# Masked attention and a max-out FFN on one core: first loads moved into the command list, V and w0 loads split, all commands ordered anew

## The chip, the core and the metric

The kernel runs on one NeuronCore of one Trainium2 chip. A core has five engines with an instruction stream each: TensorE (PE, matrix products and transposes), VectorE (DVE), ScalarE (ACT), GpSimd (POOL) and SyncE (SP, which here only issues transfers). Transfers between device memory and the on-chip memory SBUF are issued by SP, ACT or POOL and carried out by 16 DMA engines. The engines run beside each other and wait for each other by semaphores. Products land in PSUM banks and are copied or combined from there.

The metric is device time in microseconds of one execution; 8 runs of the kernel before are given.

## What is computed

Attention over 4 batches of 8 heads, 768 positions of width 64, and then a feed-forward net over the 3072 rows of 512 that come of it. Some heads (the "retrieval" heads, a flag each, read at run time) see all earlier positions; the others see the first 4 positions and the last 64.

```python
scores = scale * np.matmul(q, k.transpose(0, 1, 3, 2))
stream_keep = causal & (is_sink | in_win)          # n_sink = 4, window = 64
mask = np.where(retr, full_mask, stream_mask)      # by head
scores = np.where(mask[None], scores, -1e9)
a = np.exp(scores - max); a = a / sum(a)
x = np.matmul(a, v)                                # to (3072, 512)
h = np.maximum(np.maximum(x @ w1, x @ w2), x @ w3) # (3072, 768)
out = h @ w_out                                    # (3072, 512)
```

## The kernel before

**Tiles.** Work is cut into 16 tiles t, in the order batch, half of the 768 positions, group of four heads: t = 4 * batch + 2 * half + group. Each tile has two head pairs i = 0, 1. Scores are made transposed (keys on partitions), so that exp(scores) can be used at once as the stationary operand of the product with V; a column of ones in V gives the sums. Blocks of a tile are packed into units u (2 for the first half, 4 for the second; `UNITS`). Each half of a batch, 384 rows, is then one FFN pass: 8 passes in all.

**The order is written by hand, as a list of commands.** `PROGRAM` (L46) is a tuple of strings; at the end of the kernel each command is looked up in `do` (L647) and emits its instructions. Since every engine runs its own instructions in the order in which they were emitted, the list sets the order on every engine and on every transfer queue, and a letter in a command says which engine does a copy (`a` ACT, `d` VectorE, `p` POOL). The commands:

- `hl half hp n` (`load_first`, L298) loads k and q of n head pairs of batch 0 in fp32, from pair hp on, on SP and ACT. Before the change it can stand only in `FIRST` (L44), which is run ahead of all set-up; so does `v b half` there, and `ir`, the load of the flags.
- `ld half hp` does the same for two pairs on POOL's queue. `cast half hp ee` turns k and q of a pair into fp16 (`cast_pair`, L207; tiles kn, qn). `turnp half hp e` transposes them on PE and copies them out of PSUM into KQ (`turn_pair`, L219). This way is for batch 0 alone.
- `load b qd` loads k and q of four heads of a later batch on POOL's queue, with conversion; `turn b qd i part` transposes a quarter of them on VectorE (L258, L266).
- `load_v b half` loads V by three transfers on SP, `load_vp` on POOL (`load_v`, L280; its last two arguments pick a range of heads). `v t i ee` (`prep_v`, L497) casts V into va (L503) and makes vf (L505), V with far positions switched off for the other heads.
- `read`, `flags`, `far` spread the flags; `em hp` and `m hp` (`head_masks`, L386) make a pair of heads' mask tiles mk on VectorE (L388). Tiles 0 and 1 add the masks on PE before the exponential (L536), later ones multiply them in afterwards: `k t i u e` (`masks`, L569).
- `s t u [i] [b]` (`scores`, L517) makes the scores of a unit on PE (L552) and their exponential on ACT (L563). Two PSUM tiles named st serve in turn; with `b`, single banks are used.
- `av t i [D]` (`av`, L589): product with V (L601), reciprocal and scaling on VectorE (L609, L611). With `D` the result x is transposed by a DMA on SP (L620), otherwise by PE and a copy (`x t i e`, `turn_x`, L626). The last `x` of a half puts its FFN pass into a queue.
- `f 1 e` takes the next step of the FFN pass at the head of the queue (`ffn`, L416): 18 steps of four products of 384 columns (L437), which are copied (w0) or combined by maximum on VectorE (w1, w2; L454, L457), and then 3 output steps of six products (L473), a copy and a store, each followed by an empty step. In batch 0 all six w0 steps come first, then w1, then w2; later the three weights alternate. I call the steps of the first pass f0 to f23, so f18 is its first output, and f24 the first step of the second pass.
- `w wi` (`load_weight`, L398) loads a weight on POOL's queue, with conversion; its further arguments give a number of column parts and which of them. `idle n` (L318) multiplies zeros n times and uses nothing of it; `gate` puts a small transfer into SP's queue that waits for tile 3.

PSUM has four banks for all other products (`bank`, L169), so PE also waits until an earlier bank has been copied out. Buffers for V and for k and q of later batches exist three times each.

Of the kernel before, what the change touches and what calls it, by code (L numbers as in the profile page):

```python
# [40 lines left out]

EARLY = 0

FIRST = "hl 0 0 1, ir, hl 0 1 1, hl 0 2 2, v 0 0"  # L44

PROGRAM = (  # L46
    "read, flags, cast 0 0 pa, cast 0 1 ad, cast 0 2 pp, em 0, turnp 0 0 aa, em 3, idle 8, far",
    "ld 1 0, cast 0 3 ap, turnp 0 2 aa, em 2, turnp 0 1 dd, s 1 0 0, s 0 0 0, s 0 1 0 b, em 1",
    "w 0, turnp 0 3 d, s 0 0 1, ld 1 2, s 1 1 0 b, s 0 1 1 b, v 0 1 dd, s 1 0 1, v 1 1 dd",
    "s 1 1 1, v 0 0 dp, cast 1 1 pp, w 1, turnp 1 1 aa, cast 1 0 da, av 0 1, av 0 0, idle 2",  # L50
    "av 1 1, turnp 1 0 aa, m 0, v 1 0 pp, s 2 0 1, w 2, av 1 0, s 2 0 0, x 1 1 d, x 1 0 d",
    "x 0 1 d, x 0 0 a, s 2 1, m 1, m 2, m 3, cast 1 3 pd, f 1 d, load_vp 0 1, w 3, f 1 a, f 1 a",
    "turnp 1 3 aa, cast 1 2 dd, load 1 0, f 1 d, s 2 2, k 2 1 1 p, f 1 a, k 2 0 1 p",
    "turnp 1 2 d, f 1 d, k 2 0 2 d, f 1 a, s 3 0, k 3 0 0 d, f 1 d, f 1 d, s 2 3, k 2 1 2 p",
    "f 1 d, f 1 a, f 1 d, k 2 0 3 d, load 1 1, f 1 a, v 2 1 pp, f 1 d, f 1 d, v 2 0 ad",
    "v 3 1 ap, k 2 1 3 p, f 1 a, s 3 1 0, s 3 2 0, av 2 0 D, v 3 0 pp, s 3 1 1, f 1 d, av 2 1 D",
    "k 3 0 1 p, f 1 a, turn 1 0 0 0, k 3 1 0 p, s 3 3 0, turn 1 0 0 1, turn 1 0 1 0, s 3 2 1",
    "f 1 a, load_v 1 0, f 1 d, k 3 0 2 p, k 3 0 3 p, turn 1 0 1 1, f 1 a, k 3 1 1 p, s 3 3 1",
    "k 3 1 2 p, gate, av 3 0, s 4 0, k 3 1 3 p, turn 1 1 0 0, f 1 a, av 3 1, turn 1 1 0 1",
    "x 3 0 a, f 1 a, turn 1 1 1 1, k 4 0 0 p, x 3 1 a, f 1 d, k 4 1 0 p, s 4 1, f 1 a",  # L60
    "turn 1 1 1 0, load_v 1 1, f 1 a, v 4 0 pp, k 4 0 1 d, k 4 1 1 p, f 1 a, s 5 0, v 4 1 pp",
    "f 1 a, f 1 d, v 5 1 pd, f 1 d, f 1 d, s 5 1, load 2 1, f 1 a, v 5 0 pd, av 4 0 D, f 1 a",
    "s 6 0, k 5 0 0 d, f 1 a, load 2 0, av 4 1 D, f 1 d, k 5 0 1 d, v 6 0 pp, f 1 d, s 6 1",
    "k 5 1 1 p, f 1 d, k 5 1 0 p, f 1 d, turn 2 1 0 0, f 1 a, s 6 2, f 1 a, f 1 d, av 5 0 D",
    "f 1 d, v 6 1 pp, s 6 3, av 5 1 D, f 1 a, k 6 1 2 p, f 1 d, k 6 0 3 p, x 5 1 a, s 7 0",
    "turn 2 1 1 0, turn 2 0 1 1, f 1 a, f 1 d, turn 2 0 1 0, v 7 0 pd, f 1 a, k 6 1 1 d, s 7 1",
    "turn 2 0 0 1, f 1 a, f 1 a, k 6 0 2 d, k 6 0 1 p, f 1 a, k 6 1 3 d, f 1 d, turn 2 1 0 1",
    "f 1 a, s 7 2, load_v 2 0, f 1 d, f 1 a, f 1 a, av 6 0 D, v 7 1 ap, s 7 3, load 3 1",
    "k 7 0 1 d, k 7 1 3 p, k 7 1 1 d, av 6 1 D, f 1 a, f 1 d, f 1 a, v 9 0 dp, turn 2 0 0 0",
    "k 7 0 2 d, f 1 d, k 7 0 3 p, f 1 d, f 1 a, f 1 d, s 8 0, av 7 0 D, f 1 d, k 8 0 0 d, f 1 a",  # L70
    "k 7 1 2 p, s 8 1, load_v 3 0, k 8 0 1 p, turn 2 1 1 1, av 7 1 D, f 1 d, v 8 0 ap, s 9 0",
    "f 1 a, av 8 0 D, f 1 a, s 10 0, f 1 a, k 9 1 0 p, f 1 d, f 1 d, load_v 2 1, f 1 d, x 7 1 a",
    "s 10 1, f 1 a, f 1 d, f 1 d, k 10 0 1 d, f 1 a, v 9 1 ap, turn 3 1 0 1, f 1 a, s 9 1",
    "f 1 d, v 8 1 pp, f 1 d, k 9 0 1 d, f 1 a, k 9 1 1 d, k 8 1 1 p, k 9 0 0 p, s 10 2",
    "k 10 1 1 p, f 1 d, f 1 a, load 3 0, f 1 d, av 9 1 D, f 1 d, f 1 a, f 1 a, s 10 3, f 1 d",
    "f 1 d, k 8 1 0 p, v 10 1 dp, k 10 0 2 d, f 1 d, av 9 0 D, f 1 a, s 11 0, av 8 1 D",
    "k 10 1 2 p, f 1 a, x 9 1 d, f 1 a, s 11 1, k 10 0 3 d, v 11 0 dp, turn 3 1 1 1, f 1 a",
    "f 1 a, v 10 0 dp, turn 3 0 1 1, f 1 d, k 11 1 1 p, f 1 a, turn 3 0 1 0, k 10 1 3 d, f 1 d",
    "f 1 a, f 1 d, turn 3 0 0 1, s 11 2, f 1 d, turn 3 0 0 0, k 11 0 1 p, f 1 a, v 12 1 dd",
    "f 1 a, v 11 1 pp, f 1 a, k 11 1 2 p, s 11 3, f 1 d, k 11 1 3 d, v 12 0 dp, av 10 0 D",  # L80
    "s 12 0, k 11 0 2 p, av 10 1 D, f 1 d, f 1 a, k 12 0 0 p, k 11 0 3 p, s 12 1, f 1 d, f 1 d",
    "turn 3 1 1 0, f 1 d, k 12 0 1 p, f 1 d, av 11 0 D, turn 3 1 0 0, f 1 a, s 14 0, f 1 d",
    "f 1 d, av 11 1 D, av 12 0 D, f 1 a, f 1 d, s 13 0, k 12 1 1 d, k 12 1 0 p, f 1 d, f 1 d",
    "f 1 d, k 13 1 0 d, s 13 1, k 13 0 0 d, f 1 d, f 1 d, f 1 a, x 11 1 a, k 13 0 1 d, s 14 1",
    "load_v 3 1, f 1 a, f 1 a, f 1 a, f 1 d, f 1 a, f 1 a, v 13 0 pd, f 1 d, s 14 2, v 13 1 pd",
    "f 1 d, k 13 1 1 p, f 1 a, v 14 0 pp, f 1 a, av 13 0 D, f 1 d, k 14 0 2 d, av 13 1 D",
    "s 15 0, f 1 d, f 1 a, k 14 1 1 p, f 1 a, f 1 d, v 15 0 pd, s 14 3, x 13 1 a, f 1 a",
    "av 12 1 D, f 1 a, f 1 a, f 1 a, f 1 a, f 1 d, k 14 0 1 d, s 15 1, k 14 1 2 d, f 1 a",
# [20 lines left out]
def kernel(  # L109
# [15 lines left out]
    B, H, S, D = q.shape  # L125
# [49 lines left out]
    cast = {}  # L175
# [184 lines left out]
    far = consts.tile([P, H, 4], FP16, name="far")  # L360
# [265 lines left out]
    def turn_x(t, i, op=None):  # L626
# [87 lines left out]
```

## Time and profile before

| | us |
|---|---|
| median of 8 runs | 201.38 (199.67 to 202.95) |
| the profiled execution | 202.41 |
| its span, first to last instruction | 200.7 |
| first product on PE | 4.67 |
| first exponential of scores on ACT | 10.48 |
| first FFN product (f0) | 20.89 |
| first output product (f18) | 42.71 |
| first product of the second FFN pass (f24) | 51.01 |
| last product starts its group | 193.25 |

The page gives busy time per engine, a row of 40 slices of the span with the busy share in tenths, the clock granted to PE in tenths of full speed, and the mean share of the 16 DMA engines. Further views show the chain of work that ended last, each engine's instructions in order of time with the idle time before them and what ended it, and busy times in windows.

The largest groups, busy time and mean of one instruction:

| line, engine | what | count | busy us | mean ns |
|---|---|---|---|---|
| L563 ACT | exponentials, all shapes | 99 | 82.7 | 895 |
| L585 POOL | masks on exponentials | 51 | 54.0 | 1079 |
| L437 PE | FFN products, w0, w1, w2 | 540 | 108.4 | 327 to 333 |
| L457 VectorE | maxima, acc and hT | 90 | 49.6 | 555 |
| L473 PE | output products | 138 | 31.7 | 375 |
| L266 VectorE | transposes of k and q | 24 | 25.5 | 1133 |

Products overlap in the pipeline: one of 384 columns starts 0.16 us after the one before at full clock, so an FFN step of four takes 0.65 us and an output step 1.3. On ACT and VectorE too instructions overlap by some 0.1: exponentials of 1024 follow each other by 0.92 us, casts by 0.43 on ACT and 0.47 on VectorE.

### The profile page before, as it was taken

How to read it: one execution, taken by the hardware profiler on the slowest of the kernel's cores; microseconds unless marked ns; L12 is line 12 of the kernel's file. 1: busy time of each engine (PE TensorE's matmuls, PEld its weight loads, DVE VectorE, ACT ScalarE, POOL GpSimd, SP SyncE). 2: the span in 40 equal slices, each digit the busy share in tenths (PEclk: the TensorE clock that was granted, in tenths of full speed). 3: DMA queues.
4: the chain of work that ended last, by engine and by line, in shares of the span. 5: the costliest groups of instructions: out<-in, count | busy, mean ns of one | idle time of the engine just before them, and what ended most of it. 6: DMA issues, size and time to landing. Idle time of an engine off the chain costs nothing.

```text
span 200.7 us, 5122 instructions
## 1 busy us (share of the span) xinstructions
PE 189.3 (94%) x2059; PEld 109.3 (54%) x2059; DVE 147.5 (74%) x306; ACT 114.5 (57%) x169; POOL 98.3 (49%) x132
## 2 busy tenths in 40 slices
PE   0999699999999999999999999999999999999992
PEld 0556354656555556665465556664565466755652
DVE  3687947888589977974697989897687647665740
ACT  3599758367866797477673676435547375102021
POOL 4685954867998521925960585930253218000000
PEclk9999969999999999999999999999999999999999
DMA  5999999939799357759994140213732230014004
GB/s 179 269 259 276 211 238 213 211 78 221 195 160 205 68 178 159 118 101 178 214 213 90 39 158 4 42 23 93 195 68 42 72 127 20 5 43 151 3 0 157
DMA packets 43245, 26.48 MB, mean 132 GB/s; under 512 B 33558, under 2 KB 38230, under 8 KB 43222
## 3 DMA queue, kind: packets, MB, share of 16 engines
q1 hardware_dynamic: 37206, 15.01, 31.0%
q0 software_dynamic: 4784, 10.23, 25.8%
q10 hardware_dynamic: 1232, 0.92, 1.4%
q8 instruction: 16, 0.26, 0.6%
q14 instruction: 7, 0.06, 0.1%
HBM read 25.17 MB, written 6.29 MB: 157 GB/s over the span
## 4 chain that ended last, share of the span: by engine, by line
PE 85%; ACT 6%; DVE 3%; DMA 2%; issue 1%; POOL 1%; SPq 0%; DVEq 0%
PE yy L437 44%; PE yy L473 14%; PE st L552 11%; PE oacc L601 10%; ACT pt L563 4%; PE yst L437 3%; PE st L321 2%; DVE mk L388 1%; DMA ir<-in_is_retrieval_dram 1%; PE tr L230 1%; DMA out_dram<-ot 1%; ACT KQ L238 1%; PE yst L473 1%; ACT ot L479 1%; POOL pt L585 1%
## 5 line engine op out<-in xcount | busy, mean ns | idle before, releaser
L563 ACT ACTIVATE pt<-st 128x1024 f16<-128x1024 f32 (+3 forms) x99 | 82.7, 895 | 38.8 <-PE st L552 30.5
L585 POOL TENSOR_TENSOR pt<-pt,mk 128x512 f16<-128x512 f16 (+1 forms) x51 | 54.0, 1079 | 37.9 <-ACT pt L563 37.3
L437 PE MATMUL yy<-xT,w0t 128*128 128x384 f16 x180 | 36.7, 333 | 0.0
L437 PE MATMUL yy<-xT,w1t 128*128 128x384 f16 x180 | 36.0, 327 | 0.0
L437 PE MATMUL yy<-xT,w2t 128*128 128x384 f16 x180 | 35.7, 327 | 0.0
L457 DVE TENSOR_TENSOR acc<-yy,acc 128x384 f16<-128x384 f32 x45 | 24.9, 555 | 11.6 <-PE yy L437 5.0
L473 PE MATMUL yy<-woutt,hT 128*128 128x512 f16 (+1 forms) x138 | 31.7, 375 | 0.0
L552 PE MATMUL st<-KQ 32*128 32x384 f16 (+5 forms) x560 | 29.1, 281 | 0.4
L457 DVE TENSOR_TENSOR hT<-yy,acc 128x384 f16<-128x384 f32 x45 | 24.7, 556 | 4.2 <-PE yy L437 1.7
L601 PEld LDWEIGHTS <-pt 128*128 128x128 f16 x672 | 24.1, 97 | 5.1 <-issue 1.6
L266 DVE STREAM_TRANSPOSE KQ<-kq 128x384 f32<-128x384 f32 x24 | 25.5, 1133 | 0.0
L437 PEld LDWEIGHTS <-w0t 128*128 128x128 f16 x192 | 18.1, 99 | 13.5 <-issue 2.2
L601 PE MATMUL oacc<-va,pt 128*128 128x65 f16 x352 | 25.0, 193 | 0.4 <-POOL pt L585 0.4
L454 ACT CAST acc<-yy 128x384 f16<-128x384 f32 x29 | 13.9, 486 | 20.0 <-PE yy L437 16.8
L437 PEld LDWEIGHTS <-w2t 128*128 128x128 f16 x192 | 17.9, 98 | 11.8 <-issue 0.2
L437 PEld LDWEIGHTS <-w1t 128*128 128x128 f16 x192 | 17.1, 97 | 11.4 <-issue 1.1
L552 PEld LDWEIGHTS <-KQ 32*128 32x128 f16 (+1 forms) x560 | 12.3, 93 | 18.8 <-issue 13.0
L473 PEld LDWEIGHTS <-hT 128*128 128x128 f16 x150 | 13.9, 98 | 14.9 <-issue 0.4
L601 PE MATMUL oacc<-vf,pt 128*128 128x65 f16 x320 | 21.3, 194 | 0.0
L505 POOL TENSOR_TENSOR vf<-va,far 128x384 f16<-128x384 f16 x13 | 11.1, 853 | 19.6 <-ACT va L503 10.3
L611 DVE TENSOR_TENSOR x<-oacc,rc 128x384 f16<-128x384 f32 x32 | 17.8, 557 | 1.1
L585 DVE TENSOR_TENSOR pt<-pt,mk 128x512 f16<-128x512 f16 (+1 forms) x35 | 17.0, 508 | 0.5 <-ACT pt L563 0.5
(75 smaller groups left out, 141.1 us busy)
## 6 DMA issues: line engine op xcount, KB each, us to landing
out_dram<-ot SPq DMA_DIRECT2D x23, 256.0 KB, 2.2
vs<-in_v_dram SPq DMA_DIRECT2D x21, 256.0 KB, 4.4
kq<-in_k_dram POOLq DMA_DIRECT2D x6, 384.0 KB, 6.6
kq<-in_q_dram POOLq DMA_DIRECT2D x6, 384.0 KB, 8.4
qs<-in_q_dram ACTq DMA_DIRECT2D x4, 192.0 KB, 4.0
ks<-in_k_dram SPq DMA_DIRECT2D x4, 192.0 KB, 3.7
ks<-in_k_dram POOLq DMA_DIRECT2D x2, 384.0 KB, 6.5
qs<-in_q_dram POOLq DMA_DIRECT2D x2, 384.0 KB, 7.1
```

The lines of the kernel that those rows point to most:

```text
L266: nc.vector.transpose(out=dst.rearrange("c (p j) -> c j p", j=n)[:, j0:j1], in_=src.rearrange("c (j i) -> c j i", i=R),)
L321: nc.tensor.matmul(sink[:, 0, :], zero[:, 0:P], zero, start=True, stop=True)
L437: nc.tensor.matmul(yy[:, 0:HALF], w_t[wi][:, ks, ni * P : (ni + 1) * P], xT[b, half][ks].rearrange("p a t -> p (a t)"), start=(ks == 0), s ...
L454: copy_out[0](out=acc[ni], in_=yy[:, 0:HALF])
L457: nc.vector.tensor_tensor(out=dst, in0=yy[:, 0:HALF], in1=acc[ni], op=ALU.max)
L473: nc.tensor.matmul(yo[:, 0:n], hT[ns][:, tb * P : (tb + 1) * P], woutt[:, ns, c : c + n], start=(ns == 0), stop=(ns == NNB - 1),)
L505: vf_engine.tensor_tensor(out=vf[j][:, hs, k0:k1, 0:D], in0=vs[:, hs, 0:1] if half == 0 else va[j][:, hs, k0:k1, 0:D], in1=far[:, hs, k0:k ...
L552: nc.tensor.matmul(sts[g // m][:, g % m, c0 : c0 + n * P], KQ[rows, 0, ki * P : (ki + 1) * P], KQ[rows, 1, t0 : t0 + n * P], start=(c0 == ...
L563: nc.scalar.activation(out=pts[t, i][:, u, h0 : h0 + m, 0:w], in_=st[:, :, 0:w], func=AF.Exp, scale=sc,)
L585: engine.tensor_tensor(out=x, in0=x, in1=m, op=ALU.mult)
L601: nc.tensor.matmul(o[:, qi, hl, 0 : D + 1], pt[:, u, hl, c : c + P], vv[:, 2 * hp + hl, ki, 0 : D + 1], start=(idx == 0), stop=(idx == len ...
L611: nc.vector.tensor_tensor(out=x, in0=o[:, :, :, 0:D], in1=rc.unsqueeze(3).to_broadcast([P, HB, 2, D]), op=ALU.mult,)
```

## The change

`FIRST` keeps only k and q of pair 0 and the flags. The loads of pairs 2 and 3 (`hl 0 2 2 cs`: k on ACT, q on SP) and of pair 1 (`hl 0 1 1 ss`: both on SP) become commands of `PROGRAM`, behind the set-up and ACT's table load. The first V load becomes `load_v 0 0 0 4` and `load_v 0 0 4 4`, three transfers for heads 0 to 3 and three for heads 4 to 7. w0 is loaded as `w 0 2 0` and `w 0 2 1`, its first and last 384 columns. The other commands are the same ones, with other engine letters in many places and in another order throughout. Line numbers grow by 1. Core of the diff:

```diff
-FIRST = "hl 0 0 1, ir, hl 0 1 1, hl 0 2 2, v 0 0"
+FIRST = "hl 0 0 1, ir"
 
 PROGRAM = (
-    "read, flags, cast 0 0 pa, cast 0 1 ad, cast 0 2 pp, em 0, turnp 0 0 aa, em 3, idle 8, far",
-    "ld 1 0, cast 0 3 ap, turnp 0 2 aa, em 2, turnp 0 1 dd, s 1 0 0, s 0 0 0, s 0 1 0 b, em 1",
-    "w 0, turnp 0 3 d, s 0 0 1, ld 1 2, s 1 1 0 b, s 0 1 1 b, v 0 1 dd, s 1 0 1, v 1 1 dd",
-    "s 1 1 1, v 0 0 dp, cast 1 1 pp, w 1, turnp 1 1 aa, cast 1 0 da, av 0 1, av 0 0, idle 2",
-    "av 1 1, turnp 1 0 aa, m 0, v 1 0 pp, s 2 0 1, w 2, av 1 0, s 2 0 0, x 1 1 d, x 1 0 d",
-    "x 0 1 d, x 0 0 a, s 2 1, m 1, m 2, m 3, cast 1 3 pd, f 1 d, load_vp 0 1, w 3, f 1 a, f 1 a",
-    "turnp 1 3 aa, cast 1 2 dd, load 1 0, f 1 d, s 2 2, k 2 1 1 p, f 1 a, k 2 0 1 p",
-    "turnp 1 2 d, f 1 d, k 2 0 2 d, f 1 a, s 3 0, k 3 0 0 d, f 1 d, f 1 d, s 2 3, k 2 1 2 p",
-    "f 1 d, f 1 a, f 1 d, k 2 0 3 d, load 1 1, f 1 a, v 2 1 pp, f 1 d, f 1 d, v 2 0 ad",
-    "v 3 1 ap, k 2 1 3 p, f 1 a, s 3 1 0, s 3 2 0, av 2 0 D, v 3 0 pp, s 3 1 1, f 1 d, av 2 1 D",
-    "k 3 0 1 p, f 1 a, turn 1 0 0 0, k 3 1 0 p, s 3 3 0, turn 1 0 0 1, turn 1 0 1 0, s 3 2 1",
-    "f 1 a, load_v 1 0, f 1 d, k 3 0 2 p, k 3 0 3 p, turn 1 0 1 1, f 1 a, k 3 1 1 p, s 3 3 1",
-    "k 3 1 2 p, gate, av 3 0, s 4 0, k 3 1 3 p, turn 1 1 0 0, f 1 a, av 3 1, turn 1 1 0 1",
-    "x 3 0 a, f 1 a, turn 1 1 1 1, k 4 0 0 p, x 3 1 a, f 1 d, k 4 1 0 p, s 4 1, f 1 a",
-    "turn 1 1 1 0, load_v 1 1, f 1 a, v 4 0 pp, k 4 0 1 d, k 4 1 1 p, f 1 a, s 5 0, v 4 1 pp",
-    "f 1 a, f 1 d, v 5 1 pd, f 1 d, f 1 d, s 5 1, load 2 1, f 1 a, v 5 0 pd, av 4 0 D, f 1 a",
-    "s 6 0, k 5 0 0 d, f 1 a, load 2 0, av 4 1 D, f 1 d, k 5 0 1 d, v 6 0 pp, f 1 d, s 6 1",
-    "k 5 1 1 p, f 1 d, k 5 1 0 p, f 1 d, turn 2 1 0 0, f 1 a, s 6 2, f 1 a, f 1 d, av 5 0 D",
...
+    "read, hl 0 2 2 cs, hl 0 1 1 ss, idle 8, flags, em 0, em 3, cast 0 0 ap, idle 2",
+    "cast 0 2 aa, turnp 0 0 ad, cast 0 1 ap, cast 0 3 da, em 2, ld 1 0, s 0 0 0, turnp 0 3 da",
+    "turnp 0 1 da, far, load_v 0 0 0 4, ld 1 2, v 0 1 ad, load_v 0 0 4 4, v 0 0 ad, w 0 2 0",
+    "s 1 0 1, turnp 0 2 d, s 0 1 0 b, s 1 0 0, em 1, s 1 1 1, v 1 1 pp, cast 1 1 da, av 0 0",
+    "s 0 0 1, cast 1 0 pa, s 1 1 0 b, turnp 1 1 d, av 1 1, w 0 2 1, w 1, s 0 1 1, s 2 0 1",
+    "v 1 0 pp, av 1 0, x 0 0 d, load_vp 0 1, av 0 1, x 1 1 d, cast 1 2 pp, s 2 1 1, x 1 0 d",
+    "w 2, x 0 1 a, s 2 2 1, m 1, load 1 0, f 1 a, s 2 3 1, k 2 1 1 p, m 2, turnp 1 0 ad",
+    "k 2 1 3 p, turnp 1 2 a, f 1 d, s 2 0 0, m 0, cast 1 3 pp, s 3 0 0, f 1 d, s 2 1 0, f 1 d",
+    "s 2 2 0, f 1 a, turnp 1 3 da, w 3, k 2 0 2 d, s 2 3 0, s 3 1 0, k 2 0 1 d, k 2 0 3 p, m 3",
+    "k 2 1 2 d, v 3 0 ap, f 1 d, v 2 0 dp, f 1 d, f 1 d, load 1 1, s 3 0 1, s 3 1 1, k 3 0 0 p",
+    "f 1 a, f 1 d, f 1 d, v 2 1 dp, f 1 d, av 2 0 D, f 1 d, f 1 a, f 1 a, turn 1 0 0 0",
+    "k 3 1 1 p, k 3 0 1 p, s 3 2 0, turn 1 0 0 1, s 3 2 1, k 3 0 2 p, turn 1 0 1 0",
+    "turn 1 0 1 1, f 1 d, s 3 3 0, av 2 1 D, v 3 1 ap, s 3 3 1, f 1 a, f 1 a, load_v 1 0",
+    "k 3 1 2 d, load_v 1 1, k 3 1 3 d, k 3 0 3 p, s 4 0, k 3 1 0 p, av 3 0, gate, f 1 d, s 4 1",
+    "f 1 d, k 4 1 0 p, av 3 1, load_v 2 0, f 1 a, turn 1 1 0 0, x 3 1 a, turn 1 1 1 0, x 3 0 a",
+    "turn 1 1 1 1, f 1 a, f 1 a, f 1 a, f 1 a, turn 1 1 0 1, f 1 a, f 1 a, f 1 d, f 1 a",
+    "k 4 1 1 p, s 5 0, v 4 0 ap, k 4 0 0 d, k 5 1 0 d, f 1 a, f 1 d, f 1 a, f 1 a, k 4 0 1 p",
+    "s 5 1, load 2 0, f 1 d, v 5 0 pd, av 4 0 D, f 1 d, k 5 0 1 p, v 5 1 dp, s 6 0, f 1 d",
+    "f 1 a, f 1 d, k 5 0 0 p, f 1 a, s 6 1, v 4 1 pp, av 5 0 D, k 5 1 1 d, av 4 1 D, f 1 a",
+    "f 1 a, k 6 1 1 d, f 1 d, v 6 1 pp, av 5 1 D, s 6 2, v 6 0 dp, f 1 a, k 6 1 2 p",
...
+    "av 7 1 D, s 9 0, av 7 0 D, v 13 1 ad, f 1 a, av 8 0 D, f 1 d, s 9 1, f 1 a, s 10 0, f 1 d",
+    "av 9 0 D, f 1 a, s 10 3, f 1 a, k 10 1 2 d, turn 3 1 1 0, f 1 a, k 9 1 0 p, k 10 1 1 d",
+    "f 1 a, load_v 2 1, f 1 d, f 1 a, f 1 a, f 1 a, turn 3 1 0 1, av 9 1 D, v 11 1 pp, f 1 a",
+    "k 11 1 1 d, s 12 0, v 15 0 pd, f 1 d, k 12 0 0 p, av 11 0 D, f 1 a, s 12 1, f 1 d",
+    "k 12 0 1 p, f 1 a, k 12 1 0 p, s 13 0, f 1 a, k 12 1 1 p, f 1 d, av 11 1 D, f 1 a, s 13 1",
+    "av 12 0 D, f 1 d, k 13 0 0 p, k 13 0 1 p, k 13 1 0 p, k 13 1 1 d, s 15 0, f 1 a, f 1 d",
+    "f 1 a, x 11 1 a, f 1 d, av 13 0 D, f 1 a, f 1 d, s 15 1, f 1 a, av 12 1 D, f 1 d",
+    "av 13 1 D, s 14 0, f 1 a, f 1 d, f 1 d, f 1 a, v 14 0 pd, f 1 d, s 14 1, f 1 a, f 1 d",
+    "f 1 d, f 1 d, k 14 1 3 p, f 1 a, k 14 0 1 p, av 14 0 D, k 15 1 3 p, f 1 d, k 14 1 2 d",
+    "k 15 0 2 p, k 15 0 3 p, f 1 a, f 1 a, f 1 d, av 15 1 D, av 14 1 D, f 1 d, f 1 a, x 15 1 a",
+    "av 15 0 D, f 1 a, f 1 a, f 1 a, f 1 a, f 1 d, f 1 d, f 1 d, f 1 d, f 1 d, f 1 a, f 1 a",
...
+        hl=lambda h, hp, n, *e: load_first(int(h), int(hp), int(n), *e),
```

## The prediction

> **What bounds the kernel now.** I read the page first (busy shares, slices), then the chain of waits in order of time, then windows of 2 us, and then the timelines of single engines where those stood out.
>
> ```profile
> PE 189.3 (94%) x2059; PEld 109.3 (54%) x2059; DVE 147.5 (74%) x306; ACT 114.5 (57%) x169; POOL 98.3 (49%) x132
> PE   0999699999999999999999999999999999999992
> PEclk9999969999999999999999999999999999999999
> DMA  5999999939799357759994140213732230014004
> ```
>
> TensorE (PE) is the bound: 94% busy, and from the seventh slice to the last its row is all nines. What can be won lies in the first seven slices, and the DMA row says why they are hard: the 16 transfer engines are full there.
>
> ```profile
> 5.59 3.34 PE st L321 x8
> ...
> 10.48 5.24 ACT pt L563 x10
> ...
> 20.65 0.63 DVE mk L388 x2
> 21.28 0.48 issue
> 21.77 0.10 issue
> 21.87 2.35 DVE mk L388 x3
> 24.22 0.46 DVE qn L211
> 24.68 0.47 DVE acc L454
> 25.15 0.04 issue
> 25.20 0.33 PE tr L230 x3
> ```
>
> This is the chain of waits (start, length, what). Three pieces are not useful PE work: eight dummy products behind which PE waits for k and q (5.59), a row of exponentials on ACT (10.48), and a queue on VectorE (20.65 to 25.15): six mask instructions stand ahead of one cast, and PE's transposes wait for the cast.
>
> ```profile
> 22.00:24.00 2.00, 1.17 (x10) 0.64 (x7) 2.00 (x3) 1.90 (x4) 2.00 (x3) 1.00 1.16 209
> 24.00:26.00 2.00, 0.81 (x7) 0.55 (x7) 2.00 (x5) 0.44 (x1) 2.00 (x4) 0.95 1.15 211
> 26.00:28.00 2.00, 2.00 (x13) 0.74 (x12) 0.62 (x2) 1.04 (x3) 0.93 (x1) 0.50 1.13 278
> 28.00:30.00 2.00, 2.00 (x14) 1.37 (x13) 0.58 (x1) 1.31 (x3) 0.99 (x1) 0.70 1.04 209
> ```
>
> Columns: window, length, busy PE, PE weight load, DVE, ACT, POOL, granted clock, DMA share, GB/s. The wait leaves PE idle, and afterwards the clock is 0.50 and 0.70 though PE is busy all through. From the PE timeline: 2.02 us idle before 25.20, and about 3.4 us at half clock, so 1.7 us more. Before that PE stood until 4.67 and was slow until 8.8.
>
> **What the Trainium skill says.** "TensorE: Matmul & The Clock Gate", Part 1: PE runs at half clock until it has been busy for about 3.4 us, the windows run free, and an idle one throws it back. The trace agrees: the eight dummy products took 0.42 us each, transposes after 8.8 come 0.055 apart, and the 2.02 us gap was followed by the half clock. "SBUF — State Buffer", "SBUF: two separate sides": VectorE's two-port modes and GpSimd lock each other out. The trace agrees: a mask instruction of L388 takes 0.28 at 5.62, 0.6 at 20.6 and 1.47 at 22.75, while POOL issues transfers. "DMA: Bandwidth & Descriptors", "Issuing engines are not separate DMA queues": all issuers share the 16 engines. The trace agrees: the DMA share is over 1.0 from 4 to 40 us.
>
> **The change, part by part.** Counts of products are the same (2060 in the build), so the time moves only by waits. I follow four milestones: first exponential, first FFN product (f0), first output product (f18), first product of the second FFN (f24). Before, by the PE and ACT timelines: 10.48, 20.89, 42.71, 51.01.
>
> *Start.* The eight dummy products go ahead of everything on PE. They need only the zeroed tile (ready at 1.2): 8 x 0.42 ends at 4.8 instead of 8.8. The flags product follows (its input is ready at 4.63), two more dummies end at 5.7. Transposes of pair 0 then end at 6.1. ACT issues one load, then the table load (1.28) and warm (0.2), then two loads of k for pairs 2 and 3. The build's waits show that the second of these waits for the first q load (a completion semaphore used again; today SP pays this wait, 1.7 us). Loads land 3.2 to 4.6 us after issue in the trace. So the q load issued at 0.80 lands near 4.1, ACT casts k of pair 0 to 5.1, and then waits for the k load issued at 2.8, near 6.7. On ACT, with 0.43 per cast or copy: cast, cast, copy of pair 0's KQ end at 8.1, two casts at 8.95: **first exponential 8.95**, 1.5 earlier. Its scores need the KQ copy (8.1) and PE 0.33.
>
> *ACT becomes the bound to about 29.* ACT now also does two copies and two casts of V (4 x 0.43) ahead of the second exponential: 9.87 to 11.6. V for these is issued by head halves from 4.1 on, and landed 4.4 us after issue today, so it is there by 10. What is left of the first half's exponentials is 3 x 0.92, 4 x 0.28, 2 x 0.5 (spacings in the ACT timeline), plus two casts 0.86: 17.35. Before, the same row ended at 16.4. The last av then runs at 17.4 (0.37); behind x of the av before it VectorE makes its reciprocal and x to 19.0, PE turns it (0.17), and ACT, with two exponentials (0.92) in between, copies xT (0.43): **f0 at 19.7**, 1.2 earlier. The split of w0 is what allows that: up to the end of its first half 4.3 MB have to move, of the whole 4.7, and today's windows sum to these at 18.0 and 19.3. From 17.35 to the last of ten exponentials pairs ACT has 8 x 0.92, 2 x 0.72, and 7 copies x 0.43: 29.2. PE works 8.9 us in that time, in small gaps; the cover of ACT's extra work, PE's queue, is gone there. PE reaches f6, behind the tenth one's scores, at about 28.8 (29.86 before), with 1.1 us more of scores behind it.
>
> *VectorE from 27.65 to f18.* Behind the last KQ copy stand, before the output product: 3 masks of pt x 0.38, 2 of L388 at 0.55, 1 copy 0.47, 2 casts of V x 0.45, 12 maxima x 0.47, 2 of reciprocal and x 0.71, 4 transposes of L266 x 0.95: 14.5, so 42.1. PE's own work gives 41.9. **f18 at 42.1**, and PE has by then 1.75 us done that it did after f18 before (one av 0.94, scores 0.57 and 0.26). From there PE has three outputs 3.9, av 0.94, scores 0.34, transposes 0.34: **f24 at 47.6**, against 51.01. Raw gain 3.4.
>
> *What I take off.* (1) The mask instructions m 1 and m 2 stand again behind xT and ahead of a KQ copy that s 2 0 and ACT wait for, while POOL issues w2 and two kq loads: by the rows 0.6 and 1.47 that copy is 0.5 to 1.6 late; I take 1.0. (2) m 3, beside POOL's work in the VectorE chain: 0 to 0.9, I take 0.3. (3) Semaphore steps ("issue", 0.04 each in the chain) at some eight handovers: 0.3. (4) Later, PE work between the last av of a half and its FFN (steps between them, by the durations above) falls from 7.3, 7.1 and 5.9 us to 3.9 each in the fourth, sixth and eighth half. It must cover reciprocal and x (0.76) and the DMA transpose (2.7 to landing): 3.5. So 0.4 us is left per case if VectorE is late by more than that; 0 to 2 together, I take 0.4. Sum 2.0.
>
> *At nothing.* w1, V half 1, w2 and w_out are issued in the order w1, V, w2, kq, w_out. The bytes ahead of each, read against today's cumulated windows, give landings near 23, 27, 30 and 37; they are needed at 28.8, 29, 34 and 42. If DMA slips by 4 us the cover goes, w_out last. V for later batches on SP earlier (load_v 2 0 behind the gate) holds SP's queue only for a buffer whose reader runs near 39; behind it stand outputs, not transposes. Casts and masks moved between engines after 51: summed with the rows' durations, VectorE keeps less than 1.6 us of backlog per six FFN steps (2.5 before), ACT and POOL are unchanged within 4 us in all. No lower bound below nothing: PE has 0.4 us of waits after 51 to be won.
>
> So 3.4 - 2.0 = 1.4. The profiled execution: 202.41 - 1.4 = 201.0. The median of the eight runs is 201.38, 1.03 under the profiled one; **200.0** against it.
>
> **Rivals.** *The clock stays down (slower).* PE's dummies end at 5.7, and from 6.45 to about 12 it has some 2.6 us of work, 46%. If that counts as idle, PE runs at half clock. PE has 6.4 us of full-speed work between 9 and 17.35, ACT 8.4: 2.0 of slack. A half-clock window of 3.4 us costs 1.7. One is hidden; two cost 1.4; from the third on the whole 1.4 is gone and it turns: 201.4 + 1.7 = 203.1, four 204.8. For it: the drop after 25 us today. Against: 15.5 to 20.9, about 75% busy, kept the clock. *Nothing taken off.* VectorE's masks find POOL quiet and PE gains 3.4: 198.0. For it: masks are split in three groups instead of one; against: POOL issues as many loads. *It doesn't start earlier.* ACT's k loads land at 8.1 as the last k load today did: all of ACT's row moves 1.4 later, and the gain is 0: 201.4.
>
> **How the numbers follow.** The forecast's case 0.42 (its parts give 198.6 to 201.3), nothing taken off 0.15, no earlier start 0.18, clock 0.15, and 0.10 for a wait in the 2000 moved products that no row shows, as large as today's at 25 (2.0 idle plus 1.7): 202 to 205. The range 197.8 to 204.2 leaves out the ends. 1% is 2 us, about what can be told from no change. Faster by over 1% (under 199.4): all of the second case and two fifths of the first, 0.32; within 1%: the rest of the first and the case without an earlier start, but 0.02 of it, 0.41; slower: the clock and the unseen wait, with those 0.02, 0.27.
>
> **What would show it.** Right: dummies from about 1.4; first exponential near 9; ACT with hardly a gap from 8 to 29; no idle of 2 us on PE around 23; f18 near 42 and f24 near 48. Wrong: a granted clock of 0.5 anywhere between 6 and 20; PE waiting for L266 or L388 before f18; waits for DMA transposes at the starts of the FFNs of the fourth, sixth and eighth half.

## The result, and the profile after

| | us |
|---|---|
| after, median of 22 runs | 202.11 (200.72 to 204.17) |
| before beside it, median of 59 runs | 200.57 |
| ratio after to before | 1.0083, interval 1.0063 to 1.0103 |
| profiled execution of after, and its span | 201.89, 200.2 |

The change makes the kernel 0.8% slower; 200.0, against a median of 201.38 before, was forecast. The ratio leaves out executions over 1.5% above the fastest of their kernel, on both sides; the medians of all give 1.0077. Line numbers are one higher after the change.

The page of the changed kernel: busy shares, then the slices of PE, its clock and the transfers.

```profile
PE 190.1 (95%) x2059; PEld 108.3 (54%) x2059; DVE 150.2 (75%) x301; ACT 115.5 (58%) x170; POOL 104.4 (52%) x135
PE   7399899999999999999999999999999999999993
PEclk9969999999999999999999999999999999999999
DMA  5989999999998489993675530012440130124004
```

PE starts earlier (the first digit was 0), then stands (the 3). The dip of the clock has moved from the sixth slice to the third, that is from 25 us to about 12. PE is no less busy than before: what is lost is mostly not idle time on this page, but products at half clock and small waits.

The chain of waits of the changed kernel from its start, and PE's timeline there (in brackets: idle time before, and what ended it):

```profile
0.80 3.46 DMA qs<-in_q_dram
4.26 0.02 issue
4.29 5.12 DMA ks<-in_k_dram
```

```profile
7.07 0.39 PE L553 MATMUL st<-KQ 64*128 64x384 f16 x4 [0.61 <-DVE KQ L239]
10.11 0.34 PE L231 MATMUL tr<-ident,kn 128*128 128x128 f16 x3 [2.65 <-DVE kn L212]
```

ACT's second load of k, that of pair 3, waits until the first q has landed, is issued at 4.29 and lands at 9.40. PE waits 2.65 us for VectorE's cast of it. (ACT's first exponential ends at the same moment, so this trace alone can't tell the two apart; with V loaded whole, a run below, the exponential ends at 9.28, the load lands at 10.00 and the cast starts at 10.09: it follows the load.) Then the windows (length; busy PE, PE weight load, DVE, ACT, POOL; clock; DMA share; GB/s) read:

```profile
10.00:12.00 2.00, 1.86 (x25) 1.46 (x26) 1.90 (x8) 1.34 (x4) 0.42 (x1) 0.95 1.05 267
12.00:14.00 2.00, 2.00 (x14) 0.96 (x13) 2.00 (x5) 1.81 (x4) 2.00 (x4) 0.50 0.64 203
14.00:16.00 2.00, 2.00 (x24) 0.92 (x20) 0.81 (x3) 1.56 (x3) 2.00 (x5) 0.70 0.85 251
```

PE is busy throughout, at half clock. The transfer share falls to 0.64 just then: POOL waits for q until 8.26 and for `far` until 12.01, and issues its loads late (w0 at 14.03; before, it was at 10.3).

**Where time is lost.** A PE command takes the same time in all runs at full clock: an FFN step 0.65, an output step 1.30, an `av` 0.94 or 0.37, scores by their width. I add these along each list, and subtract the sum from the time at which the trace has the first output product of a pass. The rest is what PE has lost so far (computed from the traces; the constants are alike for all rows, so differences between rows count, not the rows' own size):

| lost up to the outputs of pass | 1st | 2nd | 4th | 5th | 8th |
|---|---|---|---|---|---|
| before, the execution of the prediction | 15.2 | 16.9 | 18.2 | 18.8 | 19.6 |
| before, a second execution | 12.7 | 14.5 | 15.8 | 16.4 | 17.2 |
| after | 14.5 | 15.0 | 16.5 | 18.4 | 19.2 |

Two things stand out. The kernel before lost 2.4 us more in the execution that was profiled for the prediction than in another, all of it ahead of the first outputs. And the changed kernel, against that second one, has lost 1.8 more at its first outputs, wins most of it back until the second (0.5 is left there, 0.7 at 110 us), and loses 1.3 more between the outputs of the 4th and 5th pass, 110 to 134 us.

### The profile page after: what moved, and what is told of

It reads as the page before. It is cut to its first block, busy times and chain, and to the rows that moved or that the text cites. A ratio compares the mean times of both kernels' runs of the same rounds, so it can differ in the third digit from the quotient of the medians.

```text
span 200.2 us, 5127 instructions
## 1 busy us (share of the span) xinstructions
PE 190.1 (95%) x2059; PEld 108.3 (54%) x2059; DVE 150.2 (75%) x301; ACT 115.5 (58%) x170; POOL 104.4 (52%) x135
## 4 chain that ended last, share of the span: by engine, by line
PE 79%; ACT 5%; POOL 5%; DMA 4%; DVE 4%; issue 2%; DVEq 0%; POOLq 0%
PE yy L438 39%; PE yy L474 14%; PE st L553 10%; PE oacc L602 9%; ACT pt L564 3%; POOL pt L586 3%; PE yst L438 3%; DMA ks<-in_k_dram 3%; DMA qs<-in_q_dram 2%; PE st L537 1%; POOL vf L506 1%; PE yst L474 1%; PE tr L231 1%; DVE vf L506 1%; DVE x L612 1%
## 5 line engine op out<-in xcount | busy, mean ns | idle before, releaser
L586 POOL TENSOR_TENSOR pt<-pt,mk 128x512 f16<-128x512 f16 (+1 forms) x60 | 63.8, 1087 | 39.5 <-ACT pt L564 35.2
L438 PEld LDWEIGHTS <-w0t 128*128 128x128 f16 x192 | 17.5, 98 | 13.4 <-issue 2.0
L438 PEld LDWEIGHTS <-w1t 128*128 128x128 f16 x192 | 17.6, 98 | 12.7 <-issue 1.6
L480 ACT COPY ot<-yy 128x512 f32<-128x512 f32 x14 | 8.2, 587 | 22.0 <-PE yy L474 10.7
L455 ACT CAST acc<-yy 128x384 f16<-128x384 f32 x24 | 11.6, 482 | 15.6 <-PE yy L438 15.3
L480 DVE COPY ot<-yy 128x512 f32<-128x512 f32 (+1 forms) x9 | 5.9, 661 | 12.3 <-PE yy L474 12.3
```

The lines of the kernel that those rows point to most:

```text
L438: nc.tensor.matmul(yy[:, 0:HALF], w_t[wi][:, ks, ni * P : (ni + 1) * P], xT[b, half][ks].rearrange("p a t -> p (a t)"), start=(ks == 0), s ...
L455: copy_out[0](out=acc[ni], in_=yy[:, 0:HALF])
L480: op(out=ot[:, c : c + n], in_=yo[:, 0:n])
L586: engine.tensor_tensor(out=x, in0=x, in1=m, op=ALU.mult)
```

## The experiments

Each ratio is to runs of the kernel before on the same chip, with its interval.

### Was the stall of the kernel before its usual course?

The kernel before, unchanged, in two more executions.

> The kernel before, unchanged, to see a second profiled execution. Theory A (the stall of 2.02 us at 23 and the half clock behind it belong to every execution): the trace shows them again and the second FFN pass begins near 51.0. Theory B (they belong to the one execution that was shown, which took 202.41 against a median of 200.57): no idle of 2 us on PE there, clock 1.0 from 24 to 30, second FFN pass near 49.2, and so the changed kernel's start, 49.4, gains nothing.

> The kernel before, a third look. The execution that the prediction was built on had six mask instructions on VectorE taking 3.65 us from 20.57 on, 2.02 us of idle PE behind them and the half clock after that. If that is the usual course, it is here again, and the second FFN pass starts near 51. If the other look is the usual one, the masks take 2.3 to 2.6, PE idles 0.7 to 1.0, the clock stays at 1.00 and the second pass starts at 48.4 to 49.0.

200.05 and 199.82 us. VectorE's six mask instructions of L388, and PE's wait behind them, first in the execution of the prediction, then in the second and third:

```profile
20.57 3.65 DVE L388 TENSOR_SCALAR mk<-kept,least 128x512 f16<-128x512 f16 x6
25.20 0.33 PE L230 MATMUL tr<-ident,qn 128*128 128x128 f16 x3 [2.02 <-DVE acc L454]
```

```profile
20.84 2.34 DVE L388 TENSOR_SCALAR mk<-kept,least 128x512 f16<-128x512 f16 x6
24.16 0.33 PE L230 MATMUL tr<-ident,qn 128*128 128x128 f16 x3 [0.71 <-DVE acc L454]
```

```profile
20.52 1.91 DVE L388 TENSOR_SCALAR mk<-kept,least 128x512 f16<-128x512 f16 x6
23.84 0.33 PE L230 MATMUL tr<-ident,qn 128*128 128x128 f16 x3 [0.71 <-DVE acc L454]
```

The same instructions took 3.65, 2.34 and 1.91 us, and PE waited 2.02, 0.71 and 0.71. Of the 1.3 us between the first two, 1.1 is a single instruction, the sixth: 1.47 against 0.34. POOL issues the load of w_out beside it in both, so what made it long in the one stays open. In the third, POOL issues no transfer until 22.23, while the last of the six runs. The second execution's windows after the wait (columns as above):

```profile
24.00:26.00 2.00, 1.84 (x18) 0.99 (x18) 1.58 (x4) 1.15 (x3) 2.00 (x4) 1.00 1.16 213
26.00:28.00 2.00, 2.00 (x17) 1.17 (x16) 1.20 (x2) 1.81 (x3) 1.51 (x2) 1.00 1.12 276
```

The clock stays at 1.00. The second FFN pass starts at 48.55 and 48.41, not at 51.01 (PE's timelines of the two, then of the changed kernel):

```profile
48.55 1.75 PE L437 MATMUL yy<-xT,w0t 128*128 128x384 f16 x9
```

```profile
48.41 1.92 PE L437 MATMUL yy<-xT,w0t 128*128 128x384 f16 x10
```

```profile
49.41 3.41 PE L438 MATMUL yy<-xT,w0t 128*128 128x384 f16 x20
```

From there to the first outputs of the last pass all three executions of the kernel before need 142.1 us (these outputs start at 193.09 in the execution of the prediction, not at 193.25 as its table has it). So the stall that was to be won is a wait of 0.7 us in these two, and costs 2.4 us more only on some executions: of 157 executions of the kernel before for which the clock is listed, 13 had a mean clock of 0.992 or less, and they are the 13 longest, 202.1 to 203.4 us. The one profiled for the prediction (202.41, clock 0.989) was of that kind. In the 59 executions beside the result such times were more frequent: 15 took 202.1 us or more, 3 of them among the eight that the prediction had; their clock is not listed.

### The first loads, and V for the sixth FFN pass

First loads back ahead of the set-up:

```diff
-FIRST = "hl 0 0 1, ir"
+FIRST = "hl 0 0 1, ir, hl 0 1 1, hl 0 2 2"
-    "read, hl 0 2 2 cs, hl 0 1 1 ss, idle 8, ..."
+    "read, idle 8, ..."
```

> The changed kernel with the first loads of k and q put back ahead of all set-up, on their old queues (V and w0 stay split, all else as changed). Theory late k (ACT's second k load waited for the first q load to land, landed at 9.40, and PE stood 2.65 us and then ran at half clock): pair 3's k is there by 8.2, PE's idle shrinks to 1.3 or less, no half clock at 12 to 15, the second FFN pass starts 0.8 to 1.5 us earlier than 49.4 and the time falls as much. Rival (ACT's row binds from 8 to 29 whatever arrives): ACT's casts begin no earlier, since four loads now stand ahead of its table load, and the time stays within 0.4 us.

1.0063 (1.0038 to 1.0088): the step is in the right direction, though its interval overlaps that of the changed kernel (1.0063 to 1.0103). POOL issues w0 earlier and f0 comes 0.43 earlier (21.31), but PE now stands 1.70 us at 8.8, for a copy of KQ that ACT does late, and the clock halves all the same.

V of batch 2, second half, earlier on SP (`load_v 2 1` behind `v 8 1 pp`; twice, the second time with more runs):

```diff
-    "... v 8 1 pp, s 10 2, ... f 1 a, load_v 2 1, f 1 d, f 1 a, ..., v 11 1 pp, ..."
+    "... v 8 1 pp, load_v 2 1, s 10 2, ... f 1 a, f 1 d, f 1 a, ..., v 11 1 pp, ..."
```

> The changed kernel with the V load of batch 2, second half, issued 7 FFN steps earlier on SP, right behind the last reader of its buffer. Theory late V (POOL stood 10.6 us for this V, and its masks and casts then delayed VectorE and PE until 132): POOL's wait at 102 to 112 falls under 3 us and the time falls by 0.6 to 1.3 us against the changed kernel, to about 201. Rival (POOL's lateness hides behind PE, the loss after 51 is elsewhere): no change within 0.3 us.

> The changed kernel with load_v 2 1 issued some ten FFN steps earlier, right behind v 8 1 pp, once more with more runs. Theory 1 (V late for POOL costs 0.65 us between 112 and 121 and nothing takes its place): a ratio of 1.004 to 1.007 against 1.0083 for the changed kernel. Theory 2 (the slack is taken up elsewhere): 1.008 to 1.012.

1.0128 (1.0075 to 1.0181) in six runs, 1.0073 (1.0039 to 1.0106) in fifteen. Alone, its effect on the time cannot be told from none. What it does in the trace is plain. The timeline of the changed kernel there, POOL and VectorE:

```profile
112.57 0.50 POOL L504 CAST va<-vs 128x384 f16<-128x384 f32 x1 [10.59 <-DMA vs<-in_v_dram]
...
113.94 3.50 POOL L586 TENSOR_TENSOR pt<-pt,mk 128x512 f16<-128x512 f16 x3
...
115.20 1.23 DVE L504 CAST va<-vs 128x384 f16<-128x384 f32 x1
116.53 1.33 DVE L506 TENSOR_TENSOR vf<-va,far 128x384 f16<-128x384 f16 x1
```

POOL waits 10.6 us for V, and its row of masks then runs just when VectorE has its own cast and vf of V. PE loses 0.65 us behind it (between 116 and 120.7). With V earlier (first of the two runs), VectorE's timeline has the same instructions as:

```profile
115.87 0.40 DVE L504 CAST va<-vs 128x384 f16<-128x384 f32 x1
116.37 0.56 DVE L506 TENSOR_TENSOR vf<-va,far 128x384 f16<-128x384 f16 x1
```

0.40 and 0.56 instead of 1.23 and 1.33, with POOL's masks over at 114; PE loses nothing there. In the two profiled executions with this edit the second FFN pass started 0.5 and 0.8 us later than in that of the changed kernel, so their ends don't show it. Of the fifteen, six have a mean clock of 0.981 to 0.983 and took 202.49 us or more, a larger share than in the changed kernel (5 of 23, below); the median of the nine others is 201.49, against 201.76 there.

Both edits together:

> Both edits of the two runs above. If late V and late k are separate losses, their gains add: 1.4 to 2.8 us under the changed kernel, 199.3 to 200.7, at or a little under the kernel before. If either is hidden, the sum is that of the other alone.

1.0047 (1.0028 to 1.0067).

### VectorE beside POOL's masks at 130 us

```diff
-    "k 11 1 1 d, s 12 0, v 15 0 pd, f 1 d, ..."
+    "k 11 1 1 d, s 12 0, f 1 d, ..."
-    "... x 13 1 a, f 1 d, v 15 1 pp, f 1 a, ..."
+    "... x 13 1 a, f 1 d, v 15 1 pp, v 15 0 pd, f 1 a, ..."
```

> The changed kernel with one command moved: v 15 0 pd from behind s 12 0 to behind v 15 1 pp, some 33 FFN steps later. Theory 1 (VectorE's vf instruction runs beside POOL's row of masks and takes 1.50 us instead of 0.55, after waiting 0.40 for POOL's cast; the maxima behind it are late and PE waits 0.50 for a bank): PE's wait at 132 and the 0.65 us that it loses there go, and nothing else changes: 201.3 to 201.6 us. Theory 2 (PE at 132 waits for its new scores or for POOL's masks and only the label of the wait is VectorE): the loss stays, 202.0 to 202.3.

The timeline of all engines in the changed kernel, from 129.5 to 132.3:

```profile
129.53 0.70 POOL L504 CAST va<-vs 128x384 f16<-128x384 f32 x1
...
130.20 3.20 POOL L586 TENSOR_TENSOR pt<-pt,mk 128x512 f16<-128x512 f16 x3
130.27 1.50 DVE L506 TENSOR_TENSOR vf<-va,far 128x384 f16<-128x384 f16 x1 [0.40 <-POOL va L504]
...
131.69 0.54 DVE L458 TENSOR_TENSOR acc<-yy,acc 128x384 f16<-128x384 f32 x1
...
132.29 0.81 PE L438 MATMUL yy<-xT,w1t 128*128 128x384 f16 x4 [0.50 <-DVE acc L458]
```

VectorE waits 0.40 for POOL's half of `v 15 0 pd`, then 1.50 instead of 0.55 beside POOL's row of masks; the maximum behind it frees a bank late. With the command moved, PE at the same place:

```profile
131.18 0.82 PE L438 MATMUL yy<-xT,w0t 128*128 128x384 f16 x4
131.84 0.81 PE L438 MATMUL yy<-xT,w1t 128*128 128x384 f16 x4
```

No wait. 1.0062 (1.0044 to 1.0081), 201.66: 0.002 less in the ratio than the changed kernel, 0.4 us and somewhat less than expected, and the intervals overlap. In its trace 0.26 us came back as a wait for a DMA transpose at 96; I found nothing in the edit that explains it.

All three edits together:

> First loads issued as before the change, load_v 2 1 earlier, and v 15 0 later, all three at once; the rest as in the changed kernel. If the three causes add: 0.5 (first loads), 0.65 (V late for POOL at 112), 0.65 (VectorE at 132) off 202.1, so 200.2 to 200.6, level with the kernel before (within 0.2%). If the two later losses are one and the same slack, 200.9 to 201.3.

1.0004 (0.9965 to 1.0043). By this ratio the slowdown is gone, though the interval is wide and the median of all 13 executions, 200.84, is 0.3% above the kernel before. Three later kernels that hold the same edits, each with something more, narrow it. The trace is that of the fastest execution (199.41, no half clock at the start; 11 of the 13 have a mean clock of 0.991 or less). Its lost time is 14.0 at the second outputs, 15.3 at the fourth, 15.9 at the fifth and 16.8 at the eighth.

### Is the half clock at the start a cost?

Dummy products where PE stood:

```diff
-    "... em 2, ld 1 0, s 0 0 0, turnp 0 3 da",
+    "... em 2, ld 1 0, s 0 0 0, idle 12, turnp 0 3 da",
```

> The changed kernel with twelve more dummy products on PE behind its first scores, where PE now stands 2.65 us (7.5 to 10.1) waiting for k of pair 3. Nothing else waits for them. Theory 1 (the clock): the pause alone brings the half clock of 12 to 15, so the granted clock stays 1.00 through 30 us, the 1.4 us that PE loses between 12.15 and 15.2 fall to under 0.3, the mean clock rises from 0.990 to 0.997, and the start of the second FFN pass comes 0.5 to 1.2 us earlier: 201.0 to 201.6 us. Theory 2 (ACT bounds this stretch): the clock stays up too, but the exponentials follow each other as before, and the time is unchanged within 0.3 us: 201.8 to 202.4.

The dummies fill the time from 7.4 to 10.0. In the windows where the changed kernel was at half clock this one reads:

```profile
12.00:14.00 2.00, 1.72 (x18) 0.79 (x17) 2.00 (x5) 2.00 (x5) 2.00 (x5) 1.00 0.74 181
14.00:16.00 2.00, 1.83 (x27) 1.06 (x26) 1.05 (x3) 1.98 (x4) 2.00 (x5) 1.00 0.79 284
```

The clock stays at 1.00, f0 comes at 20.96 instead of 21.74, and the time is 1.0101 (1.0062 to 1.0139): no gain. PE's timeline says where it went:

```profile
44.44 0.82 PE L474 MATMUL yy<-woutt,hT 128*128 128x512 f16 x3 [1.12 <-DMA woutt<-in_moe_w_out_dram]
```

The faster start runs into w_out, which lands at 44.4. In the changed kernel it landed at 42.8, 1.0 us before it was used; in the second execution of the kernel before at 35.5. So w_out next, ahead of k and q of batch 1:

```diff
-    "w 2, x 0 1 a, s 2 2 1, m 1, load 1 0, f 1 a, ..."
+    "w 2, x 0 1 a, s 2 2 1, m 1, w 3, load 1 0, f 1 a, ..."
-    "s 2 2 0, f 1 a, turnp 1 3 da, w 3, k 2 0 2 d, ..."
+    "s 2 2 0, f 1 a, turnp 1 3 da, k 2 0 2 d, ..."
```

> The changed kernel with the twelve dummy products of the run before and with the load of w_out issued ahead of k and q of batch 1 instead of behind them. With the dummies alone the clock stayed up and PE reached f0 0.78 us earlier, but w_out landed at 44.4 and PE waited 1.12 us for it. Theory 1 (transfers are the limit there, w_out being last): w_out lands 3 us or more earlier, the wait at 44 goes, f18 comes near 43.1, and 0.5 to 0.8 us are won against the changed kernel: 201.3 to 201.7, 0.9 or more under the run with dummies alone. Theory 2 (the transfers that are now later bring the same wait back at the turns of k and q of batch 1): 202.0 to 202.6.

No gain either: 1.015 (1.0092 to 1.0208) in four runs. Its timeline, VectorE and then PE:

```profile
40.56 4.08 DVE L267 STREAM_TRANSPOSE KQ<-kq 128x384 f32<-128x384 f32 x4 [2.98 <-DMA kq<-in_k_dram]
...
44.69 0.52 PE L553 MATMUL st<-KQ 32*128 32x384 f16 x8 [3.21 <-DVE KQ L267]
```

w_out is there in time, and now k of batch 1 lands at 40.5, VectorE waits 2.98 for it and PE 3.21 for VectorE. The transfers of the first 45 us have no slack in the changed order; what gets ahead makes the next one late.

With the three edits in place, dummies ahead of the first scores:

```diff
-    "... em 2, ld 1 0, s 0 0 0, ..."
+    "... em 2, ld 1 0, idle 9, s 0 0 0, ..."
```

> As the run with all three causes removed, and with nine more dummy products ahead of the first scores, where PE waits for the copy of KQ. Clock theory: no half clock from 9.7 to 13.5, 0.4 to 1.0 us below that run: 199.3 to 200.0, that is 0.998 to 0.995 of the kernel before. If ACT bounds the start: within 0.3 us of that run.

1.0007 (0.9985 to 1.0029): no difference from the run without them that these intervals show. The half clock of the changed kernel is real (3.41 us, from 11.79 to 15.20), but one such stretch is not what makes it slow. The run with the first loads put back says the same without dummies: its six executions with a mean clock of 0.997 or more have a median of 201.31, its ten of 0.989 to 0.992 one of 201.26. Two stretches are another matter. In V whole, below, whose mean clock is 0.98, half clock lasts 6.83 us (10.12 to 16.95). Of 23 executions of the changed kernel, five have a mean clock of 0.980 to 0.983 and took 202.89 to 204.17; the 17 of 0.988 to 0.992 have a median of 201.76. Whether the second stretch costs this, or something that keeps PE waiting costs both, no run here separates.

### The two splits by themselves

```diff
-    "... far, load_v 0 0 0 4, ld 1 2, v 0 1 ad, load_v 0 0 4 4, v 0 0 ad, ..."
+    "... far, load_v 0 0, ld 1 2, v 0 1 ad, v 0 0 ad, ..."
```

> The changed kernel with its first V load in three transfers of eight heads instead of six of four heads. ACT casts V of tile 0 at 11.40 without a wait in the changed kernel. Theory 1 (the split is needed to have V there): the casts on ACT wait until 12 or later, all exponentials behind them move, and the time rises by 0.3 to 1.0 us: 202.4 to 203.1. Theory 2 (V has slack, and fewer issues on SP and fewer packets beside k and q even help): 201.6 to 202.3.

```diff
-    "... v 0 0 ad, w 0 2 0",
+    "... v 0 0 ad, w 0",
-    "... av 1 1, w 0 2 1, w 1, ..."
+    "... av 1 1, w 1, ..."
```

> The changed kernel with w0 loaded whole at the place of its first half. In the changed kernel the first half is issued at 14.0 and lands at 20.9, f0 starts at 21.74. Theory 1 (the split carries the early FFN): w0 lands at 22.5 to 24 and PE waits 0.5 to 2 us for it, of which 0.3 to 1.0 stay at the end: 202.4 to 203.1. Theory 2 (ACT is the bound until 29, PE fills in with the scores behind): 201.8 to 202.3.

V whole: 1.0159 (1.0102 to 1.0216), f0 at 23.48. The first casts of V start at 12.6 instead of 11.4, k of pair 3 comes later too (PE waits 3.08 for it). In the new order the split of V seems worth more than expected, though the intervals just touch. w0 whole: 1.0133 (1.0073 to 1.0192) in four runs, which cannot be told from the changed kernel. PE's wait is there,

```profile
22.09 0.82 PE L438 MATMUL yy<-xT,w0t 128*128 128x384 f16 x4 [0.80 <-DMA w0t<-in_moe_w_dram]
```

but at f18 only 0.13 us of it are left (43.93 against 43.80).

### Can the order beat both?

With the three edits, ACT's copy of KQ moved ahead of two casts, and its casts of V behind an exponential; and then, in addition, seven dummies in PE's remaining pauses.

```diff
-    "cast 0 2 aa, turnp 0 0 ad, ..., ld 1 0, s 0 0 0, turnp 0 3 da",
+    "turnp 0 0 ad, cast 0 2 aa, ..., ld 1 0, s 0 0 0, turnp 0 3 da",
-    "..., ld 1 2, v 0 1 ad, load_v 0 0 4 4, v 0 0 ad, w 0 2 0",
-    "s 1 0 1, turnp 0 2 d, ..."
+    "..., ld 1 2, load_v 0 0 4 4, w 0 2 0",
+    "s 1 0 1, v 0 1 ad, v 0 0 ad, turnp 0 2 d, ..."
```

> As the run with all three causes removed (first loads, earlier V, later v 15 0), and on ACT the KQ copy of pair 0 ahead of the casts of pair 2, and the casts of V behind the exponential of s 1 0 1 instead of ahead of it. In that run ACT waited 0.69 us for V with exponentials ready behind it. If ACT bounds the start: first exponential from 8.73 to 8.6 or earlier, second exponential from 12.02 to 10.4, f0 0.5 to 0.9 us earlier, and the end 0.4 to 0.9 earlier: 199.5 to 200.1, a ratio of 0.995 to 0.999 to the kernel before. If PE, its clock or the transfers bound it: no gain, ratio 0.999 to 1.003.

> As the run with the three causes removed and ACT's order changed, with three dummy products ahead of the first scores and four behind them, where PE waited 0.91 and 1.08 us. Clock theory: the mean clock is 0.997 or more in nearly all runs, the runs at 0.98 to 0.99 go, and the ratio to the kernel before is 0.995 to 0.999. If ACT and the transfers bound the start: 0.999 to 1.003 as without them.

1.0002 (0.9981 to 1.0023) and 0.9995 (0.9974 to 1.0016). The dummies do for the clock what was expected (0.997 or more in 21 of 22 runs), and nothing for the time that these intervals show. Mended, the new order is as fast as the old one; no version here beats the kernel before.

## Why the prediction was wrong

**The step that failed is the conversion of the gain.** The stall was booked as if every execution had it. "Raw gain 3.4" was counted against f24 at 51.01, and "202.41 - 1.4 = 201.0", "1.03 under the profiled one; 200.0" moved the whole to the median. But 2.4 us of the 51.01 were the 2.0 us stall and the half clock, which the two other executions do not have, nor, by their clock, most of the 157: f24 is at 48.55 and 48.41 in those two. The excess of the profiled execution over the median and the gain that I booked were the same microseconds, and I took off 1.03 for the first while keeping 3.4 of the second. Measured against 51.01 the changed kernel's f24, 49.41, is 1.6 earlier, and 3.4 less take-offs 1 to 3 is 1.8; against the usual f24 the change loses 0.9 to 1.0 at this point.

**The milestones of the changed kernel** were nearer:

| | predicted | measured |
|---|---|---|
| first exponential | 8.95 | 8.40 |
| second exponential | 11.6 | 12.23 |
| f0 | 19.7 | 21.74 |
| f6 | 28.8 | 29.87 |
| f18 | 42.1 | 43.80 |
| f24 | 47.6, with take-offs 1 to 3 49.2 | 49.41 |

The sum at f24 fits within 0.2, but not by its parts. f0 was 2.0 late before any of the masks of take-off 1 could act. One term behind it is a k load on ACT. I gave a time for k of pair 2 (6.7), which landed at 4.8; ACT then waited for k of pair 1, which comes on SP:

```profile
4.76 0.93 ACT L212 CAST kn<-ks 128x384 f16<-128x384 f32 x2 [1.95 <-DMA qs<-in_q_dram]
7.57 0.51 ACT L212 CAST kn<-ks 128x384 f16<-128x384 f32 x1 [1.09 <-DMA ks<-in_k_dram]
```

For k of pair 3, whose wait for the first q load I had seen, I gave none. It was issued at 4.29 and took 5.1 us to land (in the trace of before such loads took 3.2 to 5.0, not to 4.6), and PE's transposes waited for it until 10.11. Then came the half clock, the rival that I gave 0.15. The two don't explain all: in the trace with all three edits the first loads are early and no half clock comes, and f0 is at 20.70, still 1.0 after the 19.7. And the first half of w0, for which I took 18.0, landed at 20.6 in the changed kernel, so f0 could not have come at 19.7 there. From f0 on, ACT's row and PE's queue absorbed 1.0 of the 2.0 by f6.

**Take-off 4 and "at nothing".** For all that comes after f24 I took 0.4, for late DMA transposes. Measured: 143.4 us (49.41 to 192.77) against 142.1, so 1.2 to 1.3. The transposes cost little (no wait for one in the changed kernel's trace, 0.2 to 0.5 at 95 to 97 in five of its variants). What cost was under "at nothing": I looked at the V loads that move forward (load_v 2 0), not at load_v 2 1, which moves behind two DMA transposes on SP and leaves POOL waiting 10.6 us; and I summed VectorE's work with the durations that its instructions had before, 0.4 to 0.56, where beside POOL's masks they take 1.2 to 1.5. The Trainium skill page that the prediction itself named, "SBUF — State Buffer", "SBUF: two separate sides", says that VectorE and GpSimd take the shared ports as an exclusive lock; I used it for the start only. The trace agrees here too: 0.55 for vf alone, 1.33 and 1.50 beside POOL.

**Sum.** 0.9 lost until f24 and 1.2 later make 2.1 against the second execution's trace; the medians differ by 1.5. The traces of the mended kernels show both later losses (at 112 and at 130) gone and their ratios are 0.9995 to 1.0007. How much each of the three edits is worth alone (0.001 to 0.002 in the ratio; for V, six runs gave more than the changed kernel and fifteen less) lies within the intervals; only their sum is shown.

**Rivals.** "The clock stays down" named an event that came, and the 46% of work that it asked about is a share that does let the clock fall (see the end). Its price for one stretch of half clock, hidden in PE's slack, fits too: filling the pause kept the clock and won no time. Its price for two, 1.4, is near the 1.5 between the medians of the executions with two and with one, though the cause of that difference is not shown. The 203.1 that it forecast asks for a third; the changed kernel is at 202.11, mostly with one. "It doesn't start earlier" holds for f0, not for ACT's first exponential (8.40, 2 us earlier than before): f0 came 0.6 to 0.9 later than in the two other executions of the kernel before (21.16 and 20.85). That DMA might slip and the cover go, "w_out last", was exactly what the dummies ran into; I had w_out near 37 and 5 us of cover; it landed at 42.85, and 1.0 was left.

## What to carry to other kernels

Before a stall of a profile is booked as gain, ask whether the profiled execution is longer than the median: the excess sits somewhere, and it may be that very stall. Where an order is dense, one limit hides the next (here the clock, then w_out, then k of batch 1), so a pause that is filled need not bring time. Price a VectorE instruction that reads and writes SBUF with what POOL does at that moment, and look for the place where a late load moves POOL's row onto it.

## What the runs showed of the hardware

- Pauses of PE and the clock: in the traces of these kernels the clock halved during, or up to 1.7 us after, waits of 1.70 (first loads as before), 2.02 (before), 2.65 (after) and 3.08 us (V whole); it stayed up after 0.71 (before, two executions) and 1.24 us (all three edits, though most executions of that kernel have a lower mean clock than the profiled one). Each of these stretches of half clock lasted 3.41 us, that of V whole twice as long.
- The length of the wait alone does not decide. In the traces the clock's records change on a grid of 3.41 us steps, and each half clock begins behind a step in which PE was busy for less than half: 48% in the changed kernel (8.38 to 11.79), 41% before (22.39 to 25.80), 45% with the first loads as before (6.47 to 9.88), 21% with V whole (6.71 to 10.12). With all three edits a step of 58% (5.97 to 9.38) kept full clock. Over all 17 traces, up to 190 us, 48% is the highest share with a fall behind it and 55% the lowest without; in the tail of w0 whole a step of 47% had none. The Trainium skill, "TensorE: Matmul & The Clock Gate", Part 1, gives an idle window of about 3.4 us, which runs free: the length agrees, but here a window need not be idle.
- Products that use nothing keep the clock: twelve of 512 columns in a pause of 2.65 us, 0.22 us each, held it at 1.00 through 16 us.
- VectorE beside POOL's row of masks: a cast of V from fp32 took 1.23 us instead of 0.40, vf 1.33 and 1.50 instead of 0.55.
- The same six mask instructions on VectorE took 1.91, 2.34 and 3.65 us in three executions of the same program: 1.91 with POOL issuing no transfer until the last of them ran, 2.34 and 3.65 with POOL issuing loads all through.
